# Reordering the last pass of an attention backward kernel: dV chunks ahead of dK, other tile choice in the opening, another tail

## The chip, the cores and the metric

The kernel runs on one core of one Trainium2 chip. The metric is the time on the device in microseconds (us). Most executions agree within 0.3%. Different sets of runs were taken on different chips, so every comparison below is with runs of the kernel before from the same set.

## The reference, cut to what matters

The forward function is two layers, each attention with one query token over a cached K and V (2 batches, 4 K/V heads, 16384 positions, 128 columns; 8 query heads to a K/V head) and an MLP; both layers use the same weights and the same cache. The kernel computes the output and the gradients of nine inputs.

```python
x = x + _A_ref(_layernorm(x), A_k_cache, A_v_cache, A_wq, A_wo)   # layer 0
x = x + _B_ref(_layernorm(x), B_w1, B_b1, B_w2, B_b2)
x = x + _A_ref(_layernorm(x), A_k_cache, A_v_cache, A_wq, A_wo)   # layer 1
x = x + _B_ref(_layernorm(x), B_w1, B_b1, B_w2, B_b2)
...
_out, _vjp = jax.vjp(_f, A_x, A_k_cache, A_v_cache, A_wq, A_wo, B_w1, B_b1, B_w2, B_b2)
```

The gradients of K and V (outputs 2 and 3) have the size of the cache, 33.6 MB each, in bf16. Most of the kernel's stores are these two.

## The kernel before

The last pass goes once more over K and V. The cache is cut into 32 chunks of 1 MB, four to each of eight (batch, head) groups. In the pass: V chunks are loaded and transposed to get the scores' gradient dS of layer 0; K chunks are loaded and multiplied with dS to get dq; the chunks of dV (which need nothing of this pass's loads) and of dK (which need dS) are computed and stored; and weight gradients ("fill") are computed and stored in between. At the end the last dq gives the last quarter of dWq (output 4), the products with Wq, and through a layer norm's backward the gradient of x (output 1; "dx" below).

A store or load has "landed" when its last byte has arrived. All of it shares one pool of 1 MB tiles. A tile becomes free either because it was read (`by_read`) or because a store was issued from it (`by_store`); the second kind can only be written once the store has landed.

```python
    def new_home():                       # a tile for results
        return (by_read or by_store).popleft()

    def load_tile():                      # a tile for the next load
        return (by_store or by_read).popleft()

    def store(out_ap, view, tile_):
        nc.gpsimd.dma_start(out_ap, view)
        by_store.append(tile_)
    ...
    def pump(most, spare):
        while jobs and len(open_loads) < most and n_free() > spare:
            load_next()
```

The pass is a loop over steps `m`. A step transposes half a chunk of V, and computes one half of a dV chunk and one half of a dK chunk where the two tables say so. `v_at` starts dV chunk `i` at step `2i - 3`, so the last (31) at step 59; `k_at` starts the last dK at step 58. Scores end with step 56.

```python
    v_at = {2 * i - 3: i for i in range(2, NC)}
    k_at = {(i if i < NCH else 2 * i - NCH): i for i in range(NC)}
    ...
    while 2 * m < NS + 12 or late or fill or late_pe or m <= max(v_at) + 2:
        ...                               # transposes, scores, dq, halves of dV and dK
        step_fill(1 if m < NCH else 5)    # five pieces of weight gradient
        pump(NLD + 3 if m < NCH else NLD, 3)
        m += 1
    g0 = attn_in_bwd(0, g1, dn0)          # dx, and output 1, after everything
    col_to_row_f32(g0, DJ, out_1.rearrange("b s d -> (b s) d"), "o1")
```

A weight gradient piece is a product of 4 rows (two layers by two batches) into a 128 x 512 bank, and its eviction (the copy of the finished bank into a tile, by VectorE or ScalarE):

```python
    PE.matmul(ps[:], lhsT=xrows[p:p + 4, (j0 + j) * 128:(j0 + j + 1) * 128],
              rhs=yrows[p:p + 4, y0 + c0:y0 + c0 + 512], start=True, stop=True, tile_position=(p, 0))
    evac_cast(sv_[:, j, c0:c0 + 512], ps[:], 512)
```

## Time and profile before

| | before |
|---|---|
| median of the first three runs | 1144.86 us |
| span of the profiled execution | 1140.8 us |
| bytes moved by DMA | 449.30 MB, 394 GB/s in the mean |
| last score product, last dq, last dWq store issued | 1101, 1116, 1131 us |
| output 1's store issued | 1136.7 us |

The first fence is from the page: the span, the busy time of the engines, the mean busy share of the DMA engines in 40 slices of 28.5 us, and what they moved in each.

```profile
span 1140.8 us, 39972 instructions
PE 954.6 (84%) x17567; PEld 736.6 (65%) x17567; DVE 633.4 (56%) x1347; ACT 566.2 (50%) x1418; POOL 64.7 (6%) x117
DMA  9999999998999989999999999887999999999996
GB/s 371 424 424 424 425 423 413 408 379 354 423 424 424 425 302 424 410 377 407 373 423 419 349 354 355 314 331 309 400 423 422 421 420 422 423 422 421 424 419 247
```

The reader is to see the plateau of 419 to 424 GB/s from slice 29 (counted from 0) to the one before the last: that is the last pass. The Trainium skill ("DMA: Bandwidth & Descriptors", Measured) gives 425 GB/s for a load of 16 MB on one core; this trace's plateau agrees. So the last pass moves bytes at the full rate, and only two holes are near it: slices 25 to 27 (its opening) and the last slice (its tail).

Next, the table of windows for three stretches: the opening, steps 17 to 49, and from step 49 to the end. Columns: window, its length, busy us and instructions of each engine, granted tensor clock (1 is full), mean busy share of the DMA engines (a packet counts whole where it starts, so the share can pass 1), GB/s. The steps' times are those of their first score product.

```profile
740.00:800.00 60.00, 50.94 (x779) 35.63 (x779) 46.69 (x85) 43.98 (x85) 7.19 (x13) 0.90 0.82 315
852.80:1063.80 211.00, 191.20 (x2409) 116.13 (x2407) 164.60 (x288) 152.97 (x295) 33.18 (x55) 0.81 1.02 422
1063.80:1140.75 76.95, 57.80 (x730) 33.16 (x727) 49.45 (x92) 44.43 (x84) 10.06 (x17) 0.70 0.86 357
```

The tail in windows of 3 us, same columns:

```profile
1114.00:1117.00 3.00, 1.90 (x15) 1.48 (x11) 1.71 (x5) 1.07 (x2) 0.00 (x0) 0.50 0.90 380
1117.00:1120.00 3.00, 2.33 (x12) 0.74 (x10) 1.09 (x2) 1.16 (x2) 0.00 (x0) 0.50 0.57 240
1120.00:1123.00 3.00, 2.65 (x72) 1.94 (x73) 0.89 (x3) 1.05 (x2) 0.00 (x0) 0.50 0.11 38
1123.00:1126.00 3.00, 2.19 (x11) 0.84 (x11) 2.15 (x4) 2.08 (x5) 0.53 (x1) 0.50 0.25 106
1126.00:1129.00 3.00, 3.00 (x8) 1.03 (x7) 2.49 (x4) 1.95 (x4) 1.30 (x2) 0.50 0.96 399
```

The hole of the tail is at 1117 to 1126 us: the stores that were queued have drained and the engines have not made new ones. And these lines of the timeline (start, length, engine, line, operation, tiles, idle time before and what ended it) fix the order of the tail. The first is the issue of the last load; then dq, the first dWq products, the last dWq store, and output 1:

```profile
1084.39 0.33 SPq L1193 DMA_DIRECT2D keepV<-in_A_k_cache_dram  x1
1115.95 0.17 DVE L1291 TENSOR_SCALAR dqT<-xm 128x8 f32<-128x8 f32 x1 [0.45 <-PE xm L468]
1118.13 1.86 PE L1162 MATMUL xm<-rowsA,rowsB 4*128 4x512 bf16 x4 [0.67 <-ACT rowsA L155]
1131.17 0.77 POOL L1126 DMA_DIRECT2D out_dram<-big  x1 [2.27 <-ACT big L163]
1136.65 0.55 POOL L202 DMA_DIRECT2D out_dram<-o_row  x1 [4.71 <-DVE o_row L201]
```

Last, the waits of the DMA queue that issues loads, in the opening (735 to 800 us): total, times, longest.

```profile
SPq L1193 <- DMA out_dram<-keepV: 52.0, 4, 20.5
SPq L1193 <- DMA out_dram<-keepK: 14.1, 2, 10.0
```

### The profile page before, as it was taken

To read this page: it belongs to the slowest core of one execution; us is meant where nothing else is said; L and a number is where in the kernel's file an instruction comes from. 1 tells how busy PE (TensorE), PEld (TensorE's weight loads), DVE (VectorE), ACT (ScalarE), POOL (GpSimd) and SP (SyncE) were. 2 spreads that over 40 slices of the span, in tenths; PEclk is the share of its full clock that TensorE was granted. 3 is DMA by queue.
4 is the path that set the end of the run, shared out by engine and by line. 5 is a ranking of instruction groups with operands and counts; after the bars stand their busy time and mean duration, and the time that the engine had idled before them with its cause. 6 is when DMAs were issued, how large, how long until landed. Compare 5 with 4: busy or idle time off the path is not lost. (4 is left out here: it accounts for less than half of the span.)

```text
span 1140.8 us, 39972 instructions
## 1 busy us (share of the span) xinstructions
PE 954.6 (84%) x17567; PEld 736.6 (65%) x17567; DVE 633.4 (56%) x1347; ACT 566.2 (50%) x1418; POOL 64.7 (6%) x117
## 2 busy tenths in 40 slices
PE   4988896487879885899987789988898989999885
PEld 3867674387767765888776688765555555555552
DVE  1535442133545433544845355768678868786784
ACT  0534351022535330344554444668677767776673
POOL 0000000000000000000000000001111112111111
PEclk9989785597999876999998899989779868896785
DMA  9999999998999989999999999887999999999996
GB/s 371 424 424 424 425 423 413 408 379 354 423 424 424 425 302 424 410 377 407 373 423 419 349 354 355 314 331 309 400 423 422 421 420 422 423 422 421 424 419 247
DMA packets 89130, 449.30 MB, mean 394 GB/s; under 512 B 7026, under 2 KB 7026, under 8 KB 49788
## 3 DMA queue, kind: packets, MB, share of 16 engines
q1 hardware_dynamic: 72204, 348.17, 75.4%
q0 software_dynamic: 16752, 98.59, 20.8%
q8 instruction: 137, 2.24, 0.7%
q14 instruction: 37, 0.30, 0.1%
HBM read 348.14 MB, written 98.58 MB: 392 GB/s over the span
## 5 line engine op out<-in xcount | busy, mean ns | idle before, releaser
L155 ACT COPY kT<-tp 128x512 int32<-128x512 int32 x209 | 122.8, 587 | 252.0 <-PE tp L421 243.3
L158 DVE COPY kT<-tp 128x1024 bf16<-128x1024 bf16 x159 | 108.6, 691 | 109.2 <-PE tp L421 97.3
L421 PE MATMUL tp<-ident,kv_K 128*128 128x128 bf16 x1728 | 144.5, 233 | 4.5 <-DMA kv_K<-in_A_k_cache_dram 4.4
L421 PEld LDWEIGHTS <-kv_K 128*128 128x128 bf16 x1728 | 109.6, 104 | 5.3 <-DMA kv_K<-in_A_k_cache_dram 5.2
L166 DVE CAST big<-xm 128x512 bf16<-128x512 f32 x135 | 88.1, 686 | 25.3 <-PE xm L1162 11.7
L163 ACT CAST big<-xm 128x512 bf16<-128x512 f32 x162 | 88.3, 594 | 24.6 <-PE xm L1162 12.7
L574 PEld LDWEIGHTS <-kT 128*128 128x128 bf16 x2048 | 76.6, 98 | 27.8 <-issue 21.4
L574 PE MATMUL sc<-qT_bf,kT 128*128 128x8 bf16 x2048 | 92.0, 171 | 0.3 <-issue 0.3
L538 ACT ACTIVATE e_all<-sc,negm 128x64 bf16<-128x64 f32 x256 | 77.1, 345 | 1.1 <-DVE negm L533 1.0
L307 PEld LDWEIGHTS <-wt 128*128 128x128 bf16 x1696 | 49.2, 104 | 43.7 <-issue 14.8
L421 PE MATMUL tp<-ident,kv_V 128*128 128x128 bf16 x864 | 70.1, 227 | 8.5 <-DMA kv_V<-in_A_v_cache_dram 7.6
L271 PE MATMUL wtp<-ident,wt 128*128 128x128 bf16 x928 | 73.9, 225 | 3.7 <-issue 2.5
L166 DVE CAST keepK<-xm 128x512 bf16<-128x512 f32 x91 | 59.1, 686 | 21.7 <-PE xm L1244 17.7
L453 PE MATMUL acc_all<-kv_V,e_all 128*16 128x256 bf16 x864 | 46.5, 296 | 26.4 <-DMA kv_V<-in_A_v_cache_dram 13.7
L163 ACT CAST keepK<-xm 128x512 bf16<-128x512 f32 x105 | 56.8, 594 | 23.8 <-PE xm L1244 23.1
L158 DVE COPY wT<-wtp 128x1024 bf16<-128x1024 bf16 (+1 forms) x64 | 40.7, 641 | 46.6 <-PE wtp L271 43.5
L155 ACT COPY wT<-wtp 128x512 int32<-128x512 int32 (+1 forms) x60 | 34.3, 572 | 61.7 <-PE wtp L271 47.5
L421 PEld LDWEIGHTS <-kv_V 128*128 128x128 bf16 x864 | 55.4, 102 | 10.7 <-DMA kv_V<-in_A_v_cache_dram 8.3
L166 DVE CAST keepV<-xm 128x512 bf16<-128x512 f32 (+1 forms) x80 | 52.5, 686 | 16.3 <-PE xm L1244 12.8
L163 ACT CAST keepV<-xm 128x512 bf16<-128x512 f32 (+1 forms) x93 | 50.3, 593 | 20.1 <-PE xm L1244 18.2
L538 ACT ACTIVATION_READ_ACCUMULATOR e_all<-sc,negm 128x1 f32 x256 | 60.1, 235 | 0.0
L271 PEld LDWEIGHTS <-wt 128*128 128x128 bf16 x928 | 56.3, 100 | 4.4 <-issue 3.0
(350 smaller groups left out, 1786.9 us busy)
## 6 DMA issues: line engine op xcount, KB each, us to landing
kv_K<-in_A_k_cache_dram SPq DMA_DIRECT2D x81, 1024.0 KB, 12.3
kv_V<-in_A_v_cache_dram SPq DMA_DIRECT2D x81, 1024.0 KB, 12.1
out_dram<-big POOLq DMA_DIRECT2D x36, 1024.0 KB, 18.5
wt<-in_A_wo_dram SPq DMA_DIRECT2D x32, 1024.0 KB, 10.2
wt<-in_B_w_dram SPq DMA_DIRECT2D x32, 896.0 KB, 14.2
out_dram<-keepK POOLq DMA_DIRECT2D x21, 1024.0 KB, 18.3
out_dram<-keepV POOLq DMA_DIRECT2D x19, 1024.0 KB, 15.0
wt<-in_A_wq_dram SPq DMA_DIRECT2D x16, 1024.0 KB, 9.0
```

The costliest lines, as they stand in the source:

```text
L155: S.copy(out=dst.bitcast(I32), in_=src.bitcast(I32))
L158: V.tensor_copy(out=dst, in_=src)
L163: S.copy(out=dst, in_=src)
L166: V.tensor_copy(out=dst, in_=src)
L271: PE.transpose(tp[:, o, :], wv[:, j, (o0 + o) * 128:(o0 + o + 1) * 128], ident[:])
L307: PE.matmul(fps[:, jo, :].rearrange("p (a b) -> p a b", b=2), lhsT=wv[:, j, jo * 128:(jo + 1) * 128], rhs=xT_bf[:, j0 + j, :].unsqueeze(1) ...
L421: PE.transpose(tp[:, j, :], cv[:, b * 8 + j, :], ident[:])
L453: PE.matmul(self.acc[cg:cg + 16, :], lhsT=coef(u), rhs=self.cv[:, t:t + 2, :].rearrange("p t d -> p (t d)"), start=False, stop=True, tile_ ...
L538: S.activation(out=e_all[:, g, f * half:(f + 1) * half, l, h, :], in_=sc[g][f][:, h, :].rearrange("p (a b) -> p a b", b=2), func=ACT.Exp, ...
L574: PE.matmul(sc[g][f][:, :, t % TH], lhsT=kT[:, j, :], rhs=q_bf[:, g, :], start=True, stop=True)
```

## The change

The intent: (1) in the opening, let loads take tiles that were read, not tiles whose stores have yet to land; (2) let dV run ahead of dK in the second half of the pass, so that the steps around the last dq hold less work; (3) pull the last dq one step forward; (4) compute dx and output 1 as soon as the last dq is there, in between the last dWq products; (5) give those products all 128 rows, zeros apart from four, from a tile that GpSimd fills at step 48. Cut to its core:

```diff
     def load_tile():
-        return (by_store or by_read).popleft()
+        return (by_read or by_store if opening["on"] else by_store or by_read).popleft()
...
-            if i % (2 * NCH) == NCH:
+            if i % (2 * NCH) == NCH + (2 if i < 2 * NCH else 0):
                 jobs.extend(("wq", chunks[i][0] % HKV, j) for j in (0, 4))
...
+    def in_rows(q, kv):                  # products with Wq, then dx and output 1
+        ...
+        def last():
+            V.tensor_tensor(out=dn0[:], in0=dn0[:], in1=pairs(ps, DJ), op=ALU.add)
+            g0 = attn_in_bwd(0, g1, dn0, lambda: step_fill(1), lambda: step_fill(2))
+            tail.append(lambda: col_to_row_f32(g0, DJ, out_1..., "o1", ktp.tile(...)))
+        return [lambda: part(0), lambda: part(4), last]
...
+        if kv == order[-1] % HKV:        # the last quarter of dWq
+            tail.extend(in_rows(quarters[kv], kv))
+            nz, qz = zero["t"][:, 0:D], zero["t"][:, D:2 * D]
+            late.append(rows_unit({3: (dq_all, kv * 8, HQ)}, qz, 0, 4))
+            late.extend(dw_units(nz, qz, None, [(0, 4), (4, 4)], 0, D, ...))
+            return
...
+        end = 1 if i == NC - 1 else 2
         sch.later(1, lambda: dq_quad(i, 0))
-        sch.later(2, lambda: dq_quad(i, 1))
+        sch.later(end, lambda: dq_quad(i, 1))
...
-    pump(NLD + 3, 4)
+    pump(NLD + 3, 3)
+    opening["on"] = False
-    v_at = {2 * i - 3: i for i in range(2, NC)}
+    v_at = {2 * i - 3 if i < 11 else (8 * i + 5) // 5: i for i in range(2, NC)}
...
+        if m == NS // 2 - 8:
+            zero["t"] = new_home()
+            nc.gpsimd.memset(zero["t"][:, 0:2 * D], 0.0)
+            nc.gpsimd.tensor_copy(out=zero["t"][96:100, 0:D], in_=rowsB[96:100, :])
...
-    g0 = attn_in_bwd(0, g1, dn0)
-    col_to_row_f32(g0, DJ, out_1.rearrange("b s d -> (b s) d"), "o1")
```

With the new table dV chunks take 1.6 steps from the 11th on, and the last starts at step 50 in place of 59. The rest of the diff pads small vectors so that transposes write whole tiles, and drops two fills of PSUM banks.

More of the change, by code (lines that the diff above doesn't have):

```diff
@@ L123 @@
     e_all = pers.tile([128, G, NP, 2, 8, 2], BF16, name="e_all")
-    zero1 = const.tile([128, 1], F32, name="zero1")
-    V.memset(zero1[:], 0.0)
     hot3 = const.tile([128, 128], BF16, name="hot3")
@@ L193, in row_to_col, with col_to_row_f32 @@
         V.tensor_copy(out=dst, in_=ps[:])
-    def col_to_row_f32(colT, J, dram_out, name):
-        row = wrk.tile([2, J * 128], BF16, name=name + "_row", tag="rowout")
+    def col_to_row_f32(colT, J, dram_out, name, home=None):
+        row = wrk.tile([2, J * 128], BF16, name=name + "_row", tag="rowout") if home is None else home[0:2].rearrange(
+            "p a b -> p (a b)")
         for j0 in range(0, J, 4):
@@ L201, in col_to_row_f32 @@
             V.tensor_copy(out=row[:, j0 * 128:(j0 + 4) * 128], in_=ps[0:2, :, :].rearrange("p a b -> p (a b)"))
-        nc.gpsimd.dma_start(dram_out, row[:])
+        nc.gpsimd.dma_start(dram_out, row[:, :])
     def ln_fwd(xT, name):
@@ L730, with cols4 @@
     row_to_col(r3, DJ, b2T[:], 1, "b2_ps")
-    n_all = vec.tile([128, DJ, 4], BF16, name="n_all")
-    o_all = vec.tile([128, HQ, 4], BF16, name="o_all")
-    dq_all = vec.tile([128, HQ, 4], BF16, name="dq_all")
-    gA_all = vec.tile([128, DJ, 4], BF16, name="gA_all")
-    m_all = vec.tile([128, DJ, 4], BF16, name="m_all")
-    h_all = vec.tile([128, FJ, 4], BF16, name="h_all")
-    dh_all = vec.tile([128, FJ, 4], BF16, name="dh_all")
-    gM_all = vec.tile([128, DJ, 4], BF16, name="gM_all")
-    V.tensor_copy(out=gM_all[:, :, 2:4], in_=gT4[:])
+    def cols4(J, name, used=True):
+        t = vec.tile([128, J + 7, 4], BF16, name=name)
+        V.memset(t[:, (J if used else 0):J + 7, :], 0.0)
+        return t[:]
+    n_all = cols4(DJ, "n_all")
+    o_all = cols4(HQ, "o_all")
+    dq_all = cols4(HQ, "dq_all", False)
+    gA_all = cols4(DJ, "gA_all")
+    m_all = cols4(DJ, "m_all")
+    h_all = cols4(FJ, "h_all")
+    dh_all = cols4(FJ, "dh_all")
+    gM_all = cols4(DJ, "gM_all")
+    V.tensor_copy(out=gM_all[:, 0:DJ, 2:4], in_=gT4[:])
     saved = {}
@@ L749, in attn_layer_fwd @@
         y, rstd = ln_fwd(xT[:], f"a{l}")
-        V.tensor_copy(out=n_all[:, :, lsl(l)], in_=y[:])
-        qps, _ = w_pass(A_wq, D, HD, "q_ps", xT_bf=n_all[:, :, lsl(l)])
+        V.tensor_copy(out=n_all[:, 0:DJ, lsl(l)], in_=y[:])
+        qps, _ = w_pass(A_wq, D, HD, "q_ps", xT_bf=n_all[:, 0:DJ, lsl(l)])
         qT_bf = vec.tile([128, G, 8], BF16, name=f"qT_bf{l}")
@@ L759, in attn_layer_fwd @@
         for b in range(2):
-            V.tensor_copy(out=o_all[:, :, 2 * l + b], in_=oT[:, b * HKV:(b + 1) * HKV, :].rearrange("p k r -> p (k r)"))
-        aps, _ = w_pass(A_wo, HD, D, "a_ps", xT_bf=o_all[:, :, lsl(l)])
+            V.tensor_copy(out=o_all[:, 0:HQ, 2 * l + b], in_=oT[:, b * HKV:(b + 1) * HKV, :].rearrange("p k r -> p (k r)"))
+        aps, _ = w_pass(A_wo, HD, D, "a_ps", xT_bf=o_all[:, 0:HQ, lsl(l)])
         xn = vec.tile([128, DJ, 2], F32, name=f"xA{l}")
@@ L769, in mlp_hidden @@
         y2, rstd2 = ln_fwd(y1[:], f"m{l}b")
-        V.tensor_copy(out=m_all[:, :, lsl(l)], in_=y2[:])
-        hps, _ = w_pass(B_w1, D, F, "h_ps", xT_bf=m_all[:, :, lsl(l)])
+        V.tensor_copy(out=m_all[:, 0:DJ, lsl(l)], in_=y2[:])
+        hps, _ = w_pass(B_w1, D, F, "h_ps", xT_bf=m_all[:, 0:DJ, lsl(l)])
         hpre = vec.tile([128, FJ, 2], F32, name=f"hpre{l}")
@@ L788, in mlp_hidden @@
         V.tensor_scalar(out=hh[:], in0=th[:], scalar1=1.0, scalar2=0.5, op0=ALU.add, op1=ALU.mult)
-        V.tensor_tensor(out=h_all[:, :, lsl(l)], in0=hh[:], in1=hpre[:], op=ALU.mult)
+        V.tensor_tensor(out=h_all[:, 0:FJ, lsl(l)], in0=hh[:], in1=hpre[:], op=ALU.mult)
         saved[f"m{l}"] = dict(y1=y1, rstd1=rstd1, y2=y2, rstd2=rstd2, hpre=hpre, th=th, xT=xT)
@@ L815, in mlp_hidden_bwd @@
         d1 = saved[f"m{l}"]["d1"]
-        V.tensor_tensor(out=dh_all[:, :, lsl(l)], in0=d1[:], in1=dhps[:], op=ALU.mult)
+        V.tensor_tensor(out=dh_all[:, 0:FJ, lsl(l)], in0=d1[:], in1=dhps[:], op=ALU.mult)
         if ahead is not None:
@@ L821, in mlp_in_bwd @@
         sv = saved[f"m{l}"]
-        _, dmps = w_pass(B_w1, D, F, "dm_ps", gT_bf=dh_all[:, :, lsl(l)])
+        _, dmps = w_pass(B_w1, D, F, "dm_ps", gT_bf=dh_all[:, 0:FJ, lsl(l)])
         dm = wrk.tile([128, DJ, 2], F32, name="dm_sb")
@@ L831, in attn_out_bwd @@
     def attn_out_bwd(l, gT):
-        V.tensor_copy(out=gA_all[:, :, lsl(l)], in_=gT[:])
-        _, dops = w_pass(A_wo, HD, D, "do_ps", gT_bf=gA_all[:, :, lsl(l)])
+        V.tensor_copy(out=gA_all[:, 0:DJ, lsl(l)], in_=gT[:])
+        _, dops = w_pass(A_wo, HD, D, "do_ps", gT_bf=gA_all[:, 0:DJ, lsl(l)])
         doT_bf = saved[f"a{l}"]["doT_bf"] = vec.tile([128, G, 8], BF16, name=f"doT_bf{l}")
@@ L913 @@
     mlp_hidden(0, x1)
-    fps, dhps = w_pass(B_w2, F, D, "w2a", xT_bf=h_all[:, :, lsl(0)], gT_bf=gM_all[:, :, lsl(1)])
+    fps, dhps = w_pass(B_w2, F, D, "w2a", xT_bf=h_all[:, 0:FJ, lsl(0)], gT_bf=gM_all[:, 0:DJ, lsl(1)])
     x2_ = mlp_out(0, fps)
@@ L929 @@
     V.memset(fps[:, 0:DJ * WIDE], 0.0)
-    w2b = Ahead(B_w2, F, "w2b", h_all[:, :, lsl(1)], fps)
+    w2b = Ahead(B_w2, F, "w2b", h_all[:, 0:FJ, lsl(1)], fps)
     rest = attn_bwd(1, do1, dq1, dn1, [b * HKV + kv for kv in (0, HKV - 1, *range(1, HKV - 1)) for b in range(2)
@@ L946 @@
     g2 = attn_in_bwd(1, g3, dn1, lambda: some(rest, 2), lambda: some(rest, 3))
-    V.tensor_copy(out=gM_all[:, :, lsl(0)], in_=g2[:])
+    V.tensor_copy(out=gM_all[:, 0:DJ, lsl(0)], in_=g2[:])
     dhps = px([128, 512], F32, "w2b_b")
@@ L950 @@
     for j in range(4):
-        w2b.products(j, dhps, gM_all[:, :, lsl(0)])
-    w2b.spread(gM_all[:, :, lsl(0)])
+        w2b.products(j, dhps, gM_all[:, 0:DJ, lsl(0)])
+    w2b.spread(gM_all[:, 0:DJ, lsl(0)])
     w2b.dots(4)
@@ L960 @@
                 turned += 1
-        w2b.products(j, dhps, gM_all[:, :, lsl(0)])
+        w2b.products(j, dhps, gM_all[:, 0:DJ, lsl(0)])
     copies_on(None)
@@ L1047 @@
     sv = saved["m0"]
-    _, dmps = w_pass(B_w1, D, F, "dm_ps", gT_bf=dh_all[:, :, lsl(0)],
+    _, dmps = w_pass(B_w1, D, F, "dm_ps", gT_bf=dh_all[:, 0:FJ, lsl(0)],
                      mid=lambda: (col_to_row_f32(x4, DJ, out_0.rearrange("b s d -> (b s) d"), "o0"),
@@ L1061 @@
     V.tensor_tensor(out=g1[:], in0=dx[:], in1=g2[:], op=ALU.add)
-    V.tensor_copy(out=gA_all[:, :, lsl(0)], in_=g1[:])
+    V.tensor_copy(out=gA_all[:, 0:DJ, lsl(0)], in_=g1[:])
     dops = px([128, 512], F32, "wob_b")
     for j in range(4):
-        wob.products(j, dops, gA_all[:, :, lsl(0)])
-    wob.spread(gA_all[:, :, lsl(0)])
+        wob.products(j, dops, gA_all[:, 0:DJ, lsl(0)])
+    wob.spread(gA_all[:, 0:DJ, lsl(0)])
     for j in wob.dotted:
@@ L1079 @@
             turned += 1
-        wob.products(j, dops, gA_all[:, :, lsl(0)])
+        wob.products(j, dops, gA_all[:, 0:DJ, lsl(0)])
     copies_on(None)
@@ L1086, with rows_unit @@
     rowsB = wrk.tile([128, D], BF16, name="rowsB", tag="rowout")
-    def rows_unit(srcs, dst, j0):
+    def rows_unit(srcs, dst, j0, rows=32):
         def u():
             tp = mtp()
-            n = 0
-            for i, (colT, jlo) in srcs.items():
-                jn = min(8, colT.shape[1] - jlo)
-                n = max(n, jn)
-                for j in range(jn):
-                    PE.transpose(tp[32 * i:32 * i + 4, j, :], colT[:, jlo + j, :], ident[:], tile_position=(0, 32 * i))
-            lo, hi = 32 * min(srcs), 32 * max(srcs) + 4
-            evac_bf16(dst[lo:hi, j0 * 128:(j0 + n) * 128], tp[lo:hi, 0:n, :].rearrange("p a b -> p (a b)"), n * 128)
+            upto = []
+            for i, (colT, jlo, J) in srcs.items():
+                flat = colT.rearrange("p j b -> p (j b)")
+                upto.append((min(8, J - jlo), i))
+                for j in range(upto[-1][0]):
+                    PE.transpose(tp[32 * i:32 * i + 32, j, :], flat[:, 4 * (jlo + j):4 * (jlo + j) + 32], ident[:],
+                                 tile_position=(0, 32 * i))
+            lo, done_ = min(srcs), 0
+            for n in sorted({n for n, _ in upto}):
+                first = min(i for m_, i in upto if m_ >= n)
+                p = slice(32 * first, 32 * max(srcs) + rows)
+                evac_bf16(dst[p, (j0 + done_) * 128:(j0 + n) * 128],
+                          tp[p, done_:n, :].rearrange("p a b -> p (a b)"), (n - done_) * 128)
+                done_ = n
         return Unit(u)
@@ L1120, in new_home @@
         return (by_read or by_store).popleft()
+    opening = {"on": True}
     def load_tile():
-        return (by_store or by_read).popleft()
+        return (by_read or by_store if opening["on"] else by_store or by_read).popleft()
     def store(out_ap, view, tile_):
@@ L1149, in dw_units @@
     def dw_units(xrows, yrows, i, chunks, y0, ny, out_of):
-        p = 32 * i
+        ps_, tpos = (slice(0, 128), None) if i is None else (slice(32 * i, 32 * i + 4), (32 * i, 0))
         box = {}
@@ L1161, in u @@
                         ps = mx()
-                        PE.matmul(ps[:], lhsT=xrows[p:p + 4, (j0 + j) * 128:(j0 + j + 1) * 128],
-                                  rhs=yrows[p:p + 4, y0 + c0:y0 + c0 + 512], start=True, stop=True, tile_position=(p, 0))
+                        PE.matmul(ps[:], lhsT=xrows[ps_, (j0 + j) * 128:(j0 + j + 1) * 128],
+                                  rhs=yrows[ps_, y0 + c0:y0 + c0 + 512], start=True, stop=True, tile_position=tpos)
                         evac_cast(sv_[:, j, c0:c0 + 512], ps[:], 512)
@@ L1211 @@
     fill = deque()
-    fill.append(rows_unit({0: (gM_all, 0), 1: (m_all, 0), 2: (gA_all, 0), 3: (n_all, 0)}, rowsB, 0))
+    fill.append(rows_unit({0: (gM_all, 0, DJ), 1: (m_all, 0, DJ), 2: (gA_all, 0, DJ), 3: (n_all, 0, DJ)}, rowsB, 0))
     for j0 in range(0, HQ, 8):
-        srcs = {0: (h_all, j0), 1: (dh_all, j0), 2: (o_all, j0)}
-        fill.append(rows_unit({i: v for i, v in srcs.items() if j0 < v[0].shape[1]}, rowsA, j0))
+        srcs = {0: (h_all, j0, FJ), 1: (dh_all, j0, FJ), 2: (o_all, j0, HQ)}
+        fill.append(rows_unit({i: v for i, v in srcs.items() if j0 < v[2]}, rowsA, j0))
     units = [dw_units(rowsA, rowsB, 0, list(w_chunks(F, D)), 0, D, rows_of(out_8)),
@@ L1224 @@
     fill.extend(dw_units(rowsA, rowsB, 2, list(w_chunks(HD, D)), 0, D, rows_of(out_5)))
-    late, late_pe = deque(), deque()
+    late, late_pe, tail = deque(), deque(), deque()
     def make_qm(w, g):
@@ L1260, in quarter_loads, with part @@
         late_pe.extend(q[2])
+    def in_rows(q, kv):
+        box, ps = q[4], pm_([128, 512], F32, "dn_tail")
+        def part(a):
+            for j in range(a, a + 4):
+                for o in range(8):
+                    PE.matmul(wide_out(ps, 2 * j), lhsT=box[j - j % 4][:, j % 4, o * 128:(o + 1) * 128],
+                              rhs=wide_in(dq_all[:, kv * 8 + o, 0:2]), start=(o == 0), stop=(o == 7))
+        def last():
+            V.tensor_tensor(out=dn0[:], in0=dn0[:], in1=pairs(ps, DJ), op=ALU.add)
+            g0 = attn_in_bwd(0, g1, dn0, lambda: step_fill(1), lambda: step_fill(2))
+            tail.append(lambda: col_to_row_f32(g0, DJ, out_1.rearrange("b s d -> (b s) d"), "o1",
+                                               ktp.tile([128, 8, 128], BF16, name="o1", tag="kT")))
+        return [lambda: part(0), lambda: part(4), last]
     def quarter(kv):
         quarters[kv][1]()
+        if kv == order[-1] % HKV:
+            while late_pe:
+                late_pe.popleft()()
+            tail.extend(in_rows(quarters[kv], kv))
+            nz, qz = zero["t"][:, 0:D], zero["t"][:, D:2 * D]
+            late.append(rows_unit({3: (dq_all, kv * 8, HQ)}, qz, 0, 4))
+            late.extend(dw_units(nz, qz, None, [(0, 4), (4, 4)], 0, D,
+                                 lambda j0, rb: dwq_v[:, j0:j0 + rb, kv * D:(kv + 1) * D]))
+            return
         late_pe.append(quarters[kv][3])
-        late.append(rows_unit({3: (dq_all, kv * 8)}, rowsA, kv * 8))
+        late.append(rows_unit({3: (dq_all, kv * 8, HQ)}, rowsA, kv * 8))
         late.extend(dw_units(rowsB, rowsA, 3, [(0, 4), (4, 4)], kv * D, D,
@@ L1319, in score0 @@
             open_dq(g)
-            if order.index(g) % 2 == 1:
-                quarter_loads(g % HKV)
+        if order.index(g) % 2 == 1 and c == (2 if i < 2 * NCH else 0):
+            quarter_loads(g % HKV)
         ds0(i, dps["t"][:])
+        end = 1 if i == NC - 1 else 2
         sch.later(1, lambda: dq_quad(i, 0))
-        sch.later(2, lambda: dq_quad(i, 1))
+        sch.later(end, lambda: dq_quad(i, 1))
         if c == NCH - 1:
-            sch.later(2, accs[g].evac)
-            sch.later(3, accs[g].reduce)
+            sch.later(end, accs[g].evac)
+            sch.later(end + 1, accs[g].reduce)
     def step_fill(n):
@@ L1338 @@
     TP = []
-    def fixed_tp(i):
-        t = pt([128, 8, 128], BF16, "tpm%d" % i)
-        S.copy(out=t[:].bitcast(F32), in_=zero1[:].to_broadcast([128, 512]))
-        return t
     def kept_scores(c, dp):
@@ L1386 @@
     delta(0, dl_bank, halves[0])
-    TP.extend(fixed_tp(i) for i in range(2))
+    TP.extend(pt([128, 8, 128], BF16, "tpm%d" % i) for i in range(2))
     banks["tp"] = lambda: nxt("tp", TP)
@@ L1390 @@
     sch.later(0, accs[order[0]].reduce)
-    pump(NLD + 3, 4)
-    v_at = {2 * i - 3: i for i in range(2, NC)}
+    pump(NLD + 3, 3)
+    opening["on"] = False
+    v_at = {2 * i - 3 if i < 11 else (8 * i + 5) // 5: i for i in range(2, NC)}
     k_at = {(i if i < NCH else 2 * i - NCH): i for i in range(NC)}
     NS = (NC - NCH) * NB
+    zero = {}
     m = 0
-    while 2 * m < NS + 12 or late or fill or late_pe or m <= max(v_at) + 2:
+    while 2 * m < NS + 12 or late or fill or late_pe or tail or m <= max(v_at) + 2:
         sch.s = m
@@ L1423 @@
                 score0(s - 2)
-            if late_pe and (k == 1 or s >= NS):
+            if late_pe and (k == 1 or s >= NS or len(late_pe) > 6):
                 late_pe.popleft()()
@@ L1429 @@
                     kv_pair(w, at[m_ - h], h)
+            if tail:
+                tail.popleft()()
         for f in qs:
```

## The prediction

> **What bounds the kernel now.** The page puts 449.3 MB through the DMA engines in a span of 1140.8 us; its fully busy slices read 421 to 425 GB/s. At 424 GB/s the bytes alone take 1060 us. The Trainium skill ("DMA: Bandwidth & Descriptors", Measured) has 425 GB/s for a 16 MB transfer; this trace agrees. So time can only be gained where the DMA engines idle, about 80 us in all. By the table of 10 us windows the last pass (800 to 1110 us) runs at a DMA share of 1.0. The change touches two holes:
> - Opening, 740 to 800 us: shares 0.67, 0.87, 0.94, 0.59, 0.82, 1.01, about 11 us idle. The DMA queue's own waits show why: loads queue in order behind tiles whose stores have not landed (52 us on one group of dV stores, 20.5 us at once), while tiles already read lie free.
> - Tail: shares 0.57, 0.11, 0.25 from 1117 to 1126 us, and nothing after 1138: about 11 us idle. By the timeline dq is ready at 1116, the last dWq store is issued at 1131.2, output 1 only at 1136.7.
>
> **What the change does.** No byte and no large operation is added or removed.
> 1. Reloading into read tiles first lets loads start without waiting for a landing. I estimate 3 to 4 MB pulled into the hole, but the vector and tensor engines are about 80 to 95% busy there, so perhaps 4 us survive.
> 2. dV chunks end at step 50 in place of 59. This reorders work inside a saturated stretch: worth nothing there, and it delays the last loads, because more stores go before them (estimate 4 MB, some 10 us). In return the last steps hold one product half in place of two (four evictions of 0.59 or 0.69 us on two engines, about 1.8 us), and one slot is cut from the last dq. From the last V transposes (1095) to dq should take about 14 us instead of 21.
> 3. After dq: 15 us up to the last store issue now, because dK, dV and the input products (2 us) are mixed in and dx waits for the end. Afterwards 8 to 9 us; output 1 (5 us of its own chain) goes beside it.
> 4. Zero-padded dWq: the skill ("TensorE: Matmul & The Clock Gate", Part 1) says activity in a 3.4 us window sets the clock. The trace's clock is 0.50 from 1105 on, and 4-row products take about 0.43 us there. Windows full of 4-row products are followed by a half clock here, so full-row ones may raise it; then the evictions (0.32 us a tile on two engines) bound: 1 to 2 us at most.
> 5. Costs: a fill of 2048 columns on the queue that issues stores, one tile less, about ten extra small evictions: under 1 us on the path. Removed bank fills: below 1 us.
>
> **Sum.** Opening -4, tail -7 (the delay of item 2 eats part of 14): about 1134 us. 80% range 1122 to 1142. Faster by over 2% (below 1122) 0.09, within 2% 0.90, slower 0.01.
>
> **What would show it.** Windows of 740 to 800 us with higher DMA share; the DMA share at 1.0 until some 15 us from the end; output 1 issued before the last dWq store; from dq to the last store issue 8 to 9 us; padded products near 0.22 us; byte total unchanged.
>
> **What would make it wrong.** The opening is bound by the engines, so that earlier loads only starve the stores of tiles; dV in front empties the store queue early, so that the tail has less DMA work to hide behind; the fill waits for a landing and holds up the stores.

## The result, and the profile after

The changed kernel took 1153.98 us in the median (1152.89 to 1155.21, four runs), the kernel before 1145.09 us in the same set. The ratio is 1.0074, 95% interval 1.0052 to 1.0097. Ratios are the mean time of one kernel's fast runs over that of the other's of the same rounds, so they are not quite the ratio of the medians quoted. So the change is slower by about 8.5 us: inside the 2% that counts as the same, but outside the range of the prediction and on the other side of zero. The two profiled executions differ by 11.8 us, somewhat more than that.

The page after, the same lines:

```profile
span 1152.6 us, 39956 instructions
PE 955.8 (83%) x17565; PEld 738.3 (64%) x17567; DVE 634.9 (55%) x1360; ACT 567.8 (49%) x1420; POOL 67.3 (6%) x119
DMA  9999999999999989999999999988999999999994
GB/s 373 423 425 425 424 424 412 404 359 370 424 424 418 424 306 423 389 354 407 371 419 421 350 363 342 352 321 320 391 409 413 420 419 423 410 390 418 423 420 190
```

Work and bytes are the same; what changed is when. The plateau has dents (391, 409, 390) and the last slice is emptier (190 against 247). The three stretches, at the steps' new times:

```profile
740.00:800.00 60.00, 51.42 (x757) 34.37 (x756) 44.23 (x81) 40.65 (x79) 6.63 (x12) 0.86 0.82 321
856.90:1087.60 230.70, 205.10 (x2490) 122.62 (x2488) 176.18 (x310) 164.94 (x315) 35.64 (x60) 0.80 1.01 414
1087.60:1152.58 64.98, 46.17 (x646) 28.16 (x645) 38.94 (x75) 33.69 (x67) 10.27 (x15) 0.79 0.77 318
```

This is the account of the difference between the two profiles. Step 17 comes 4.1 us later, steps 17 to 49 take 19.7 us more, and from step 49 to the end it takes 12.0 us less: 11.8 us together, the difference of the two spans. The middle moved 95.5 MB in place of 89.0 (rate times length); at 422 GB/s the 6.5 MB are 15.4 us, and the other 4.3 us are the lower rate. The end moved 6.8 MB less, and at the old rate of 357 GB/s that would have taken 58 us; it took 65, because the DMA share fell from 0.86 to 0.77. Two cautions. The profiles with the old dV order and the same pool (before, e1, f1, f2 and g3 in the table below) have middles of 210.8 to 217.0 us at 416 to 422 GB/s, so the 4.3 us lie within what profiles differ by; the bytes that came forward do not (they moved 89 to 90 MB there). And a dV chunk brings its products and evictions along with its store: PE was busy for 205.1 us of the middle in place of 191.2, 13.9 us more. No run separates the bytes from this work as what made the middle longer.

The tail after, in windows of 3 us:

```profile
1122.00:1125.00 3.00, 2.57 (x28) 1.41 (x16) 1.80 (x4) 1.35 (x3) 0.06 (x1) 0.50 0.98 412
1125.00:1128.00 3.00, 1.56 (x9) 1.05 (x11) 1.11 (x4) 0.00 (x0) 0.47 (x1) 0.50 0.90 380
1128.00:1131.00 3.00, 2.61 (x24) 0.83 (x24) 1.80 (x3) 1.62 (x3) 0.00 (x0) 0.50 0.42 175
1131.00:1134.00 3.00, 3.00 (x62) 1.92 (x59) 1.13 (x3) 1.70 (x4) 0.00 (x0) 0.50 0.08 30
1134.00:1137.00 3.00, 2.02 (x11) 0.40 (x9) 2.43 (x4) 1.82 (x5) 0.76 (x1) 0.81 0.22 90
1137.00:1140.00 3.00, 0.73 (x3) 0.34 (x4) 2.02 (x12) 0.98 (x2) 0.53 (x1) 0.76 0.99 410
1140.00:1143.00 3.00, 2.02 (x9) 0.98 (x10) 0.83 (x2) 0.00 (x0) 0.00 (x0) 0.50 0.51 216
1143.00:1146.00 3.00, 1.71 (x5) 0.30 (x2) 1.97 (x3) 1.07 (x2) 0.53 (x1) 0.60 0.02 4
```

The hole is still there, from 1128 to 1137 us, and there is a second at 1143 to 1146. The timeline shows the order of things:

```profile
1102.99 3.61 SPq L1205 DMA_DIRECT2D keepK<-in_A_k_cache_dram  x2
1121.44 1.03 PE L452 MATMUL acc_all<-keepK,dX 128*16 128x256 bf16 x16 [1.35 <-DMA keepK<-in_A_k_cache_dram]
1124.91 0.17 DVE L1329 TENSOR_SCALAR dqT<-xm 128x8 f32<-128x8 f32 x1 [0.52 <-PE xm L467]
1132.37 2.29 PE L1174 MATMUL xm<-keepK 128*128 128x512 bf16 x5
1140.21 1.01 PE L199 MATMUL o<-identf,gA 128*2 128x128 f32 x4 [1.68 <-DVE gA L912]
1142.80 1.91 PE L1174 MATMUL xm<-keepK 128*128 128x512 bf16 x4
1144.01 0.53 POOL L201 DMA_DIRECT2D out_dram<-o  x1 [5.85 <-DVE o L200]
1146.01 0.78 POOL L1138 DMA_DIRECT2D out_dram<-keepK  x1 [1.47 <-DVE keepK L164]
```

The last loads are issued at 1103 to 1106 us (before: 1084), and the tensor engine now waits 1.35 us for the last K chunk. dq is there at 1124.9 (before: 1116.0). After dq it takes 21.1 us to the last dWq store (before: 15.2): the last four padded products (1142.80) stand behind the transposes of dx in the tensor engine's program, and these wait for VectorE (1.68 us before 1140.21). Output 1 is out first, at 1144.0.

The waits of the load queue in the opening:

```profile
SPq L1205 <- DMA out_dram<-keepV: 26.7, 2, 19.8
SPq L1205 <- DMA out_dram<-keepK: 21.1, 1, 21.1
SPq L1205 <- PE acc_all L452: 8.6, 2, 7.4
SPq L1205 <- DMA out_dram<-keepxV: 8.4, 1, 8.4
```

The queue waits as long as before: 56 us for stores to land in place of 66, but 8.6 us for tiles that were still being read (third line); with the waits below 2 us that are not shown, 66 us in all in place of 67. A load takes a stored tile only where no read one is in the pool, so the read tiles that the prediction saw lying free mostly ran out. There are still stalls of 20 us, and the DMA share of the opening is 0.82 as before. (Profiles differ here: with the new opening this share lies between 0.74, in g1, and 0.86, in f3 and others.)

### The profile page after: what moved, and what is told of

Its sections match the earlier page's. It is cut to its first block, busy times and chain, and to the rows that moved or that the text cites. A ratio compares the mean times of both kernels' runs of the same rounds, so it can differ in the third digit from the quotient of the medians.

```text
span 1152.6 us, 39956 instructions
## 1 busy us (share of the span) xinstructions
PE 955.8 (83%) x17565; PEld 738.3 (64%) x17567; DVE 634.9 (55%) x1360; ACT 567.8 (49%) x1420; POOL 67.3 (6%) x119
## 3 DMA queue, kind: packets, MB, share of 16 engines
q0 software_dynamic: 16752, 98.59, 20.7%
## 5 line engine op out<-in xcount | busy, mean ns | idle before, releaser
L161 ACT CAST big<-xm 128x512 bf16<-128x512 f32 x149 | 80.8, 593 | 26.0 <-PE xm L1256 17.3
L270 PE MATMUL wtp<-ident,wt 128*128 128x128 bf16 x928 | 76.4, 230 | 3.9 <-issue 2.4
L537 ACT ACTIVATE e_all<-sc,negm 128x64 bf16<-128x64 f32 x256 | 77.1, 343 | 1.1 <-DVE negm L532 1.0
L164 DVE CAST keepV<-xm 128x512 bf16<-128x512 f32 x99 | 64.2, 685 | 15.9 <-PE xm L1256 10.5
L161 ACT CAST keepV<-xm 128x512 bf16<-128x512 f32 x107 | 58.1, 589 | 24.3 <-PE xm L1256 19.7
L452 PE MATMUL acc_all<-kv_V,e_all 128*16 128x256 bf16 x864 | 46.1, 293 | 27.5 <-DMA kv_V<-in_A_v_cache_dram 15.3
L164 DVE CAST keepK<-xm 128x512 bf16<-128x512 f32 (+1 forms) x84 | 54.9, 685 | 20.0 <-PE xm L1256 12.2
L420 PEld LDWEIGHTS <-kv_V 128*128 128x128 bf16 x864 | 56.1, 103 | 13.8 <-DMA kv_V<-in_A_v_cache_dram 11.8
L161 ACT CAST keepK<-xm 128x512 bf16<-128x512 f32 (+1 forms) x98 | 53.5, 591 | 19.4 <-PE xm L1256 10.6
## 6 DMA issues: line engine op xcount, KB each, us to landing
kv_V<-in_A_v_cache_dram SPq DMA_DIRECT2D x81, 1024.0 KB, 11.8
out_dram<-big POOLq DMA_DIRECT2D x36, 1024.0 KB, 15.4
```

The costliest lines, as they stand in the source:

```text
L161: S.copy(out=dst, in_=src)
L164: V.tensor_copy(out=dst, in_=src)
L270: PE.transpose(tp[:, o, :], wv[:, j, (o0 + o) * 128:(o0 + o + 1) * 128], ident[:])
L420: PE.transpose(tp[:, j, :], cv[:, b * 8 + j, :], ident[:])
L452: PE.matmul(self.acc[cg:cg + 16, :], lhsT=coef(u), rhs=self.cv[:, t:t + 2, :].rearrange("p t d -> p (t d)"), start=False, stop=True, tile_ ...
L537: S.activation(out=e_all[:, g, f * half:(f + 1) * half, l, h, :], in_=sc[g][f][:, h, :].rearrange("p (a b) -> p a b", b=2), func=ACT.Exp, ...
```

## The experiments

The theories. A: dV in front puts stores ahead of the last loads, so that dq is late. B: dx in front of the last dWq products costs time. C: the opening costs time. Later D: slow load packets; E, M and P: the end, the crowd in the middle, the pool of tiles. All kernels gave correct results. "Lead" is that of the last dV chunk's start against step 59; times within one profile are read from that profile; the landing of the last load is read from the trace's DMA packets. All results first:

| run | dV lead (steps) | median us; before | ratio, 95% interval | steps 17-49 us | 49 to end us | DMA share, 49 to end | last load landed, dq, last dWq store issued |
|---|---|---|---|---|---|---|---|
| before | 0 | 1145.09 | 1 | 211.0 | 77.0 | 0.86 | 1098, 1116, 1131 |
| after | 9 | 1153.98; 1145.09 | 1.0074, 1.0052-1.0097 | 230.7 | 65.0 | 0.77 | 1121, 1125, 1146 |
| f3: after again | 9 | 1151.69; 1144.67 | 1.0072, 1.0050-1.0094 | 232.0 | 63.6 | 0.75 | 1116, 1124, 1145 |
| e1: old dV order | 0 | 1144.84; 1143.06 | 1.0015, 0.9985-1.0046 | 217.0 | 73.6 | 0.84 | 1099, 1115, 1136 |
| e2: dx last | 9 | 1149.88; 1143.06 | 1.0063, 1.0036-1.0091 | 232.1 | 59.6 | 0.80 | 1116, 1124, 1138 |
| e3: old opening | 9 | 1156.44; 1143.06 | 1.0127, 1.0088-1.0166 | 236.9 | 63.7 | 0.72 | 1113, 1128, 1148 |
| e4: new dV order alone | 9 | 1153.44; 1143.06 | 1.0078, 1.0046-1.0111 | 229.2 | 63.5 | 0.81 | 1112, 1121, 1135 |
| f1: old dV order and dx last | 0 | 1144.24; 1144.67 | 1.0006, 0.9987-1.0025 | 213.6 | 77.1 | 0.86 | 1099, 1111, 1129 |
| f2: new opening alone | 0 | 1144.61; 1144.67 | 1.0006, 0.9984-1.0027 | 213.6 | 74.9 | 0.86 | 1097, 1115, 1130 |
| f4: half the lead | 4 | 1145.34; 1144.67 | 1.0015, 0.9996-1.0034 | 225.7 | 65.8 | 0.85 | 1104, 1118, 1132 |
| g1: read tiles first always | 9 | 1154.26; 1143.21 | 1.0093, 1.0065-1.0121 | 230.1 | 69.7 | 0.77 | 1124, 1129, 1151 |
| g2: dV later | -2 | 1147.25; 1143.21 | 1.0037, 1.0016-1.0058 | 216.8 | 77.8 | 0.82 | 1097, 1117, 1136 |
| g3: opening and early dq alone | 0 | 1145.87; 1143.21 | 1.0016, 0.9999-1.0032 | 210.8 | 78.4 | 0.86 | 1103, 1116, 1135 |
| g4: no zero padding | 9 | 1152.69; 1143.21 | 1.0069, 1.0041-1.0097 | 235.1 | 64.0 | 0.71 | 1110, 1127, 1148 |
| h1: last loads first | 9 | 1167.41; 1145.81 | 1.0198, 1.0174-1.0222 | 243.0 | 71.0 | 0.59 | 1113, 1141, 1162 |
| h2: one tile fewer | 0 | 1147.33; 1145.81 | 1.0025, 1.0004-1.0046 | 219.6 | 79.0 | 0.83 | 1104, 1122, 1137 |
| h3: lead made late | 9 | 1154.59; 1145.81 | 1.0080, 1.0056-1.0104 | 240.7 | 60.5 | 0.71 | 1111, 1129, 1143 |
| h4: lead made early and given up | 0 | 1147.64; 1145.81 | 1.0030, 0.9993-1.0066 | 220.0 | 71.4 | 0.83 | 1100, 1119, 1135 |

### e1: the old dV order in the changed kernel

```diff
-    v_at = {2 * i - 3 if i < 11 else (8 * i + 5) // 5: i for i in range(2, NC)}
+    v_at = {2 * i - 3: i for i in range(2, NC)}
```

> The changed kernel with the old dV order (two steps a chunk, last dV at step 59). Theory A (dV in front puts stores ahead of the last loads, so dq is late): 1143 to 1148 us, last load landing back from 1121 to about 1096 to 1103 us, DMA share and rate of 800 to 1100 us back from 411 to about 420 GB/s. Rival B (the loss is the order of work after dq, dx in front of the last dWq products): 1152 or more, from dq to the last store issue still about 21 us. Rival C (the opening): 1152 or more.

The loss is gone: 1.0015, not told from before. The last load lands at 1099 us again. From dq to the last dWq store it is still 22.0 us (1114.5 to 1136.5), and yet the kernel is not told from before, which speaks against B as the main cause. Its middle and end:

```profile
852.40:1069.40 217.00, 198.06 (x2409) 118.74 (x2407) 165.37 (x288) 154.56 (x294) 33.58 (x56) 0.76 1.01 416
1069.40:1143.04 73.64, 55.21 (x727) 32.84 (x727) 48.99 (x93) 43.57 (x83) 12.42 (x19) 0.75 0.84 351
```

One part of my expectation failed: the rate of the middle came back only to 416 GB/s.

### e2: dx and output 1 behind the loop again

```diff
             V.tensor_tensor(out=dn0[:], in0=dn0[:], in1=pairs(ps, DJ), op=ALU.add)
-            g0 = attn_in_bwd(0, g1, dn0, lambda: step_fill(1), lambda: step_fill(2))
-            tail.append(lambda: col_to_row_f32(g0, ...))
...
         m += 1
+    g0 = attn_in_bwd(0, g1, dn0)
+    col_to_row_f32(g0, DJ, out_1.rearrange("b s d -> (b s) d"), "o1", ktp.tile(...))
```

> The changed kernel with dx and output 1 moved behind the loop again, as before the change. Rival B: 1147 to 1150 us, the last dWq store issued some 5 us earlier (about 15 to 16 us after dq). Theory A alone: within 2 us of the changed kernel's 1154, because output 1 then ends last as it did before.

The last dWq store comes 14.0 us after dq instead of 21, as B said, but output 1 comes 5.3 us after that, and the time is 1.0063, against 1.0072 and 1.0074 for the changed kernel: a difference inside the intervals. (The median fell in B's range of 1147 to 1150, but the kernel before was 2 us faster in this set too.) B holds for the order of the tail and is not told from zero for the time. In the kernel before, the last dWq store landed at 1138.1 us and output 1 at 1138.3: the chain of dx was already hidden behind that landing, so there was nothing to win by moving it.

### e3: the old opening in the changed kernel

```diff
-        return (by_read or by_store if opening["on"] else by_store or by_read).popleft()
+        return (by_store or by_read).popleft()
...
-    pump(NLD + 3, 3)
+    pump(NLD + 3, 4)
```

> The changed kernel with the old rule for tiles in the opening (stored tiles first, four spare). Rival C (the opening costs time): 1150 or less. Theory A: within 2 us of 1154. My prediction had the opening worth 4 us, which would put this at 1158.

It got slower, 1.0127, with a spread of 14 us between its runs; so C falls. Taken alone this would make the opening worth about 5 us in the company of the new dV order. But e4 has the new dV order with the old opening too, and stands at 1.0078, as the changed kernel does; so that isn't shown. Alone the opening is worth nothing (f2).

### e4: the new dV order alone in the kernel before

The same one-line edit of `v_at`, the other way round.

> The kernel before with the new dV order alone. Theory A: 1150 to 1156 us, last loads landing some 15 to 25 us later than 1097, load packets slower in 800 to 1100 us (excess of about 5 us in place of 2). Rivals B and C: 1143 to 1147, no slower than before.

1.0078: the one line costs all that the whole change costs. The profiled execution was the fastest of the six (1146.4 us against a median of 1153.4), so its profile shows less of the loss than its times: the packet excess that I expected is not in it (1.4 us, where the kernel before has 1.9). Its middle and end:

```profile
851.90:1081.10 229.20, 201.74 (x2491) 120.06 (x2489) 176.19 (x311) 165.40 (x315) 35.59 (x60) 0.80 1.02 420
1081.10:1144.62 63.52, 47.84 (x647) 29.25 (x645) 39.24 (x75) 33.44 (x65) 7.65 (x13) 0.74 0.81 338
```

### f1: the old dV order and dx last in the changed kernel

Both edits, of e1 and of e2.

> The changed kernel with both suspects undone: old dV order and dx behind the loop. If the two costs add (9 us and about 4 us) and the opening keeps its gain: 1137 to 1141 us, faster than the kernel before of this chip by 2 to 6 us; last dWq store about 14 us after dq, output 1 some 5 us after that. If the opening's gain is given back in the pass: equal to before within 2 us.

Equal to before, 1.0006. So everything else of the change (opening, early dq, padding) is worth nothing together (within 3 us by the interval), and the costs do not simply add. dq comes at 1111.3, 4.6 us earlier than before, but the last dWq store only 18.1 us later, at 1129.4.

### f2: the opening alone

```diff
+    opening = {"on": True}
     def load_tile():
-        return (by_store or by_read).popleft()
+        return (by_read or by_store if opening["on"] else by_store or by_read).popleft()
...          # the first weight quarter two chunks later, three spare, opening off after it
```

> The kernel before with the opening alone (read tiles first, three spare, first weight quarter two chunks later). My prediction's item 1: 4 us faster than before. Rival (given back, because the engines set the pace of the pass once its loads are ahead): within 1.5 us of before, more bytes moved by 800 us (about +1 MB) but no more by 1000 us, and slower load packets in between.

1.0006, the rival: the interval leaves it at most 1.8 us of gain. By 800 us it had moved 312.1 MB (before: 311.2), by 900 us 353.2 (352.8), by 1000 us 395.1 (395.0): the lead was given back within 200 us. This lead of 0.9 MB is small: by 800 us the seven other profiles with the old opening lie between 309.9 and 311.6 MB, the nine others with the new one between 309.3 and 312.6. The load queue of f2 waits 66 us in all from 735 to 800 us, as in the kernel before (67): the waits that the opening was to remove are still there. The excess of its load packets from 800 to 1100 us (explained at g1) was 3.4 us (before: 1.9).

### f3: the changed kernel again, as a control

No edit.

> The changed kernel itself as a control on this chip: 1.007 to 1.010 of before.

1.0072, and a second profile of the same shape (232.0, 63.6 us), so the account above is not that of one odd execution.

### f4: half the lead

```diff
-    v_at = {2 * i - 3: i for i in range(2, NC)}
+    v_at = {2 * i - 3 if i < 11 else (9 * i - 4) // 5: i for i in range(2, NC)}
```

> The kernel before with dV chunks at 1.8 steps each in the second half (last at step 55, against 59 before and 50 in the change). Theory A with cost in proportion to the lead: 3 to 5 us slower than before, last load landing about 1103 to 1106 us. Rival (a threshold, the tail is only hit when the queue runs empty): within 1.5 us of before.

1.0015, between my two alternatives: 1.7 us, where cost in proportion to the lead (4 steps of 9, at 1.0072) would be 3.7 us, and the interval reaches 3.9. So a cost in proportion is not excluded. The last load landed at 1104 us, as theory A said. The profile shows how the cost could be lower:

```profile
851.10:1076.80 225.70, 202.68 (x2450) 120.56 (x2448) 171.87 (x302) 159.38 (x310) 34.81 (x58) 0.78 1.01 416
1076.80:1142.58 65.78, 48.76 (x688) 29.54 (x685) 43.55 (x82) 38.02 (x73) 8.40 (x15) 0.76 0.85 353
```

The end is already down to 65.8 us with 23.2 MB left to move. The full lead leaves 20.7 MB and takes 65.0. The 2.5 MB between the two are 6 us of DMA work and gave back 0.8.

### g1: read tiles first throughout

```diff
     pump(NLD + 3, 3)
-    opening["on"] = False
```

> The changed kernel with the rule of the opening kept for the whole pass: loads take read tiles first and new results take stored tiles, so that loads seldom wait for a store to land. Theory D (loads issued late, into an almost empty DMA queue, run slow packets and land late): excess of load packets from 800 to 1100 us down from about 6 to 3 us or less, last load landing before 1110 us, 1145 to 1150 us. Rival: the results now wait for landings instead and hold up the engines: 1152 or more, steps 17 to 49 no shorter than 231 us.

I had found that a load that starts on an almost empty DMA queue moves its 8 KB packets slower (last section), and the changed kernel has more of those: its load packets from 800 to 1100 us took 6.8 us more (time of all 16 DMA engines together) than at their usual length, before 1.9. g1 removes much of this (3.9 us), and the rate of the middle is 420 GB/s again. It is no faster: 1.0093. And e1, which is not told from before, still has an excess of 5.2 us. So D falls as the cause. Slow packets go with a queue that runs short.

### g2: dV two steps later

```diff
+    v_at = {2 * i - 3 if i < 11 else 2 * i - 1: i for i in range(2, NC)}
```

> The kernel before with dV chunks from the 11th on two steps later (last at step 61 in place of 59). Theory A with a slack (last loads have about 18 us to spare before dq in the kernel before): bringing them still earlier gains nothing, and two more halves are left for the end: 0 to 3 us slower than before, last load landing about 1093 to 1097 us. Rival (time in proportion to the lead of dV): 2 us faster.

1.0037: a lag costs too, a little more than I expected. The last load lands at 1097, no earlier than before, and the last dWq store is 5 us later. None of the other orders tried (full lead, half lead, this lag, and those of h3 and h4 below) beats that of the kernel before.

### g3: a candidate

The edits of f2 and the early dq (`end = 1` for the last chunk) on the kernel before.

> Candidate: the kernel before with the opening and with the last dq pulled one slot forward, nothing else. If dq four to five us earlier carries through to the end: 1139 to 1141 us, 0.3 to 0.5% faster than before. If it is used up by the tail (as in f1, where dq came at 1111 but the last dWq store 18 us later): within 0.15% of before.

1.0016: no gain. No version beats the kernel before.

### g4: no zero padding

```diff
-            nz, qz = zero["t"][:, 0:D], zero["t"][:, D:2 * D]
-            late.append(rows_unit({3: (dq_all, kv * 8, HQ)}, qz, 0, 4))
+            late.append(rows_unit({3: (dq_all, kv * 8, HQ)}, rowsA, kv * 8))
...          # four-row products as before; no filled tile
```

> The changed kernel without the zero-padded last dWq (no filled tile, four-row products as before the change). If the padding matters as I predicted (1 to 2 us): 1.5 us slower than the changed kernel, about 1.009 of before. If it does not, because products at the half clock take 0.43 us with 4 rows and with 128 alike: 1.006 to 1.008 of before.

1.0069: the padding is not seen in the time either way. The groups of instructions from 1110 us on, before and then after (count, busy us, mean ns of one), show the products to be about as long with 128 rows as with 4 (g4's own sixteen 4-row products: 619 ns):

```profile
L1162 PE MATMUL xm<-rowsA,rowsB 4*128 4x512 bf16 x16 | 7.1, 623 | 1.2 <-ACT rowsA L155 0.7 <-ACT keepK L163 0.5
```

```profile
L1174 PE MATMUL xm<-keepK 128*128 128x512 bf16 x14 | 6.6, 590 | 1.8 <-DVE keepK L156 0.9 <-ACT big L161 0.6 <-issue 0.2
```

### h1 to h4: the end, the middle, or the tiles

h1 changes the pump of the changed kernel, h2 the pool of the kernel before, h3 and h4 its dV table:

```diff
-        pump(NLD + 3 if m < NCH else NLD, 3)                                          # h1
+        pump(NLD + 3 if m < NCH or m > 40 else NLD, 1 if m > 40 else 3)
-    by_read.extend(ld.tile([128, LDW], BF16, name="big", tag="ld") for _ in range(NLD - 1))   # h2
+    by_read.extend(ld.tile([128, LDW], BF16, name="big", tag="ld") for _ in range(NLD - 2))
+    v_at = {2 * i - 3 if i < 21 else 37 + 13 * (i - 20) // 11: i ...}                 # h3
+    v_at = {... (8 * i + 5) // 5 if i < 22 else 34 + 5 * (i - 21) // 2: i ...}        # h4
```

> The changed kernel, but from step 41 on the loads may take all but one free tile and ten may be open. Theory E (the end: dq waits for the last loads): last load landing earlier than 1116 us by 5 us or more, dq and the end earlier by about as much, 1145 to 1149 us. Rival M (the crowd of stores in the middle): last load earlier or not, time within 2 us of the changed kernel (1.007 of before).

h1 got far slower, 1.0198. Its last load landed at 1113 us, earlier than in either profile of the changed kernel, and dq came at 1141, later than ever. The timeline shows why:

```profile
1045.40 1.56 ACT L161 CAST big<-xm 128x512 bf16<-128x512 f32 x3 [10.81 <-DMA out_dram<-big]
1046.03 1.56 PE L1256 MATMUL xm<-QmV,blk 32*128 32x256 bf16 x8 [11.19 <-ACT big L161]
```

The loads took the free tiles, an eviction had to wait 10.8 us for a store to land, and the tensor engine stood behind it for 11.2 us. So "dq waits for the last loads" is not by itself the cause, and tiles given to loads are taken from results. Because h1 brought a new stall in, it doesn't decide between E and M.

> The kernel before with one tile fewer in the last pass's pool. Theory P (the pool sets the depth of the DMA queue and the time with it): 3 us or more slower, stores landing sooner after their issue (median below 19 us in place of 21), more slow load packets. Rival: within 1.5 us of before; then a tile more or less does not explain the 9 us.

1.0025: one tile fewer costs about 3 us (at most 5 by the interval), at the edge between my two alternatives. The pool matters somewhat; it is not 9 us.

> The kernel before, dV in the old order up to step 37 and then hurried, last at step 50 as in the change. Theory E (the end): 6 to 10 us slower, as the full lead (e4), last load landing after 1110 us. Rival M (the middle): at most 4 us slower, since the lead lasts only for the last 12 steps.

1.0080, as E said and against M: the lead lasts for twelve steps only and costs as much as the lead from step 18 on.

```profile
851.30:1092.00 240.70, 214.19 (x2499) 126.83 (x2497) 177.47 (x311) 166.78 (x318) 35.86 (x60) 0.74 1.01 414
1092.00:1152.49 60.49, 46.19 (x640) 28.62 (x637) 38.25 (x73) 31.95 (x63) 7.24 (x13) 0.75 0.71 292
```

Its end has only 17.7 MB to move (42 us at 422 GB/s) and still takes 60.5 us.

> The kernel before with the change's lead from step 18 to 34 and then slower, last at step 59 as before. Theory E: within 2 us of before, last load landing at about 1098 us. Rival M: 4 us or more slower, with more slow load packets between steps 17 and 49.

1.0030 (0.9993 to 1.0066): about 3 us, under half the cost, which is between the two alternatives, and its interval excludes neither. Its lead is given up again by step 59. h3 is what speaks for E; with h4 it favours the reading that what counts is how much dV is left for the last steps.

## Why the prediction was wrong

The mean loss of the changed kernel is shown to come from the order of the dV chunks: taking it out removes it (e1, f1), putting it in alone makes it (e4), and the rest together is worth nothing (f1: 1.0006). How the order costs time is read from the profiles, below. Point by point:

- "What bounds the kernel now" was right: bytes are unchanged and the pass runs at 419 to 424 GB/s. What I passed over is that the tensor engine is busy for 191 of 211 us in the same stretch, so the stretch has two limits.
- "Opening -4" failed. Alone it is worth 0 (f2). The wait that it was to remove stayed: the load queue still waits 66 us (67 before), in the changed kernel and in f2, since the pool ran out of read tiles. "I estimate 3 to 4 MB pulled into the hole" came to 0.9 MB in f2, gone 200 us later, and to none in the profile of the changed kernel (310.7 MB by 800 us in place of 311.2).
- "This reorders work inside a saturated stretch: worth nothing there" failed: 6.5 MB came forward ("estimate 4 MB"), 15.4 us at 422 GB/s, and the middle took 19.7 us more, of which the end gave back 12.0.
- **The step that failed is the term "tail -7 (the delay of item 2 eats part of 14)".** It is wrong in the delay and in the part after dq. The delay was put at 10 us (and -14 with 10 back would have been -4, not -7). Measured, the last load landed 18 to 23 us later (1116 and 1121 against 1098), and the last V transposes 17.9 us later. The gain was put at 7 us for "from the last V transposes to dq" (about 14 in place of 21) and 6 us after dq. The first was there, and larger: from the third of the last chunk's four blocks, which the prediction counted from, it is 11.2 us (1113.7 to 1124.9) in place of 20.1 (1095.9 to 1116.0), 8.9 us less. The second was wrong in sign: 21.1 us after dq in place of "8 to 9", 5.9 us more than before, since dx stands ahead of the last products in the program of the engines. Together these put the last dWq store 14.8 us later, and 12.3 us of that are left at its landing (1138.1 and 1150.4). Of the two, the delay is what costs the time: undoing it alone removes the loss (e1), undoing the order after dq alone does not (e2).
- Output 1's "5 us of its own chain" beside the products had nothing to win: in the kernel before it landed 0.2 us after the last dWq store.
- "1 to 2 us at most" for the padding: not seen (g4). "Padded products near 0.22 us" failed: they start 0.42 to 0.43 us apart (1132.75 to 1134.03), as the 4-row ones do. The clock did rise for one window after five of them (1135.1 to 1138.6 us), then fell while the engine waited for dx, and rose again after the last four (from 1145.4 us), too late for any product.
- My warning "dV in front empties the store queue early, so that the tail has less DMA work to hide behind" is the reading that fits the runs best. I had named it and gave it no weight.

The mechanism that fits the profiles, argued and not shown by an experiment: from step 49 on the kernel has a chain of its own (last loads, dS, dq, dWq, landing) of some 60 to 66 us. Before, the end had 27.5 MB to move, 65 us at 422 GB/s, about as long as that chain (it took 77 us), so the two were near a balance. With half the lead (f4) the end shrank by 11 us and almost paid for the middle. With the full lead it shrank by 12 us in all, although it had 6 us less to move than with half: the end stayed at 60 to 66 us in f4, e2, e3, e4, f3, g4, after and h3, whether 23 or 18 MB were left (g1 and h1, which changed the rule for tiles, are above it with 70 and 71 us). Stores that come early are paid for in the middle and are missed at the end.

What stays open: the chain of 60 to 66 us was read from profiles and not shortened by an experiment. Whether the middle grew by the bytes or by the engines' work that came with them was not separated. The middle's lower rate (414 against 422 GB/s, 4.3 us) was not traced to a cause: g1 had 420 GB/s and won nothing, and e1 had 416 and lost nothing. And whether the 4.1 us by which step 17 comes later belong to the change isn't settled: this step comes between 848 and 857 us in the profiles of all kernels.

## What to carry to other kernels

Where a pass is full on the DMA side, as here, moving stores earlier gained nothing by itself: ask what the end will then have to hide its own chain behind, and compare the bytes left with the length of that chain. Cost a reordering at both places, where the work arrives and where it leaves; here 6.5 MB cost the middle 19.7 us and gave the end 12.0 us back. Before moving a chain out of the last place, look whether it is already hidden behind a landing.

## What the Trainium skill lacked or had wrong

- "DMA: Bandwidth & Descriptors" (Measured, and Latency and other measured facts): it has rates by size of transfer, but no time per packet of this size, and so not how packets slow down in a load that starts on an almost empty queue. Here 8 KB packets of loads take 309 to 311 ns inside a stream. Over all eighteen profiles, after 850 us, loads of such packets whose first one ran within 2.5 us of their issue took 398 ns a packet in the mean (45 loads, 312 to 496 ns), those that started more than 3.5 us after it 311 ns (494 loads). So a load issued into a short queue ran at 78% of the usual packet rate in the mean.
- "TensorE: Matmul & The Clock Gate" (Part 1): it says that the clock follows how busy the engine was in a window of 3413 ns, and gives 426.7 ns for a 512-column product at the half clock; both agree with this trace (windows of 3.413 us; padded products start 0.42 to 0.43 us apart). It gives no measure of busy by the rows and columns of the array that a product uses. In the trace of the kernel before, from 740 us on, I weighted the streamed columns of each window by the share of rows and of columns of the array that the product used. Of windows with 3200 or more such columns all 57 were followed by the full clock, of those under 2400 none of 35, whatever the clock was, and of the 25 between them 11. The other traces agree: in all eighteen together 1000 of 1001 windows and 16 of 661. Unweighted columns don't separate them (of 45 windows at full clock with 6000 to 9000 columns, 27). By this measure a 4-row product counts a thirty-second of a 128-row one, so a stretch of them leaves the clock to fall although the engine is busy.
- "TensorE: Matmul & The Clock Gate" does not say that padding such products with zero rows can raise the clock. Here, in all eight profiles with the padding the clock rose to full for 3.4 us or more at some time after dq, and in none of the ten without it (in g4 a full-clock stretch that began before dq ended 1.6 us after it). It gained no time that was seen (g4).
